# The score matmuls of an attention group and the first replacement of the search ahead of it: a change of order in a scheduled kernel

## The chip, the cores and the metric

The kernel runs on one core of a Trainium2 chip. The metric is the device time of one execution in microseconds (us). Three timed runs of the kernel before gave 1064.5, 1066.62 and 1068.95 us, median 1066.62. The profile is that of one further execution, which took 1060.82 us; its span from the first to the last instruction is 1059.1 us. The engines are named as the profile names them: PE is TensorE (matmuls), PEld its weight loads, DVE is VectorE, ACT is ScalarE, POOL is GpSimd, SP is SyncE, which issues most of the DMAs.

## The reference

Three layers follow each other; all is in float32.

```python
# attention: batch 4, 8 heads, 576 rows, head size 64; only the 32 highest scores of a row count
scores = q @ k.T / sqrt(64)
kth    = np.partition(scores, -32)[..., -32:-31]
scores = np.where(scores >= kth, scores, -1e9)
attn   = softmax(scores);  x = attn @ v          # x: 2304 tokens x 512
# a dense layer: 512 -> 2048 -> 512
h = x @ w_in;  x = (np.maximum(h, 0) + np.log1p(np.exp(-abs(h)))) @ w_out
# 8 experts, each token goes to the one with the highest gate
logits = x @ w_gate;  e = argmax(logits)
out = softmax(logits)[e] * (np.maximum(x @ w1[e], 0) @ w2[e])
```

## The kernel before

The program has two parts. `part_one` computes the attention, the dense layer and the routing of each token to its expert; `part_two` runs the experts, 256 token places at a time. The change is in `part_one`.

Attention is worked in 72 groups. A group is two tiles of 128 score rows x 576 keys. For a group, `emit_scores` issues two sets of matmuls through `emit_qk`: the first set gives keys 0 to 255 into the PSUM tile `sa`, which ScalarE copies to the SBUF tile `s` (L416); the second set gives the other 320 keys into the PSUM tile `sb`. Both sets are matmuls of line L406. There is one buffer of `sa` and one of `sb`. So the `sa` matmuls of a group wait for the copy L416 of the group ahead, and the `sb` matmuls wait for the copy L452 of the group ahead, which is the last reader of `sb`.

`emit_softmax` then finds the 32nd highest score of each row. Six VectorE instructions fold the scores pairwise (L446 to L451; L446 is the first and needs both `s` from L416 and `sb`), ScalarE copies `sb` to `s` (L452), and then VectorE alternates between taking the eight highest values (MAX8, L456 and L472) and replacing them by a very small number (MATCH_REPLACE8, L468), three times. The result `kth` goes to ScalarE (`kths`, L479), which with GpSimd makes the masked exponentials: L480 on ScalarE, L481 on GpSimd, the exponential L482 on ScalarE, then two 16-bit halves (L490 to L492) and a DMA transpose to `pT` (L494). Three groups later `emit_av` multiplies `pT` with v (L509, L511) and VectorE divides by the sums (L533 to L536).

When all groups of a set of token tiles are done, the set becomes a unit of the dense layer. `layer1` (L596) and `layer2` (L636) are TensorE's large matmuls; between them ScalarE computes exp and ln (L610, L611). Such a step has twelve L596 matmuls, followed later by two or four L636 entries, and the main loop emits 1.7 steps per attention group once units are ready; what is left over follows after the last group. The loads of q, k and v for later heads (L326), sums of their absolute values for a later check (L335) and their 16-bit halves (L367, L380) are made ahead of need on the same engines. The weights of the dense layer are decoded during the first groups on ScalarE, VectorE and GpSimd (L247 to L260). L664 to L705 route the finished tokens.

No order is written out by hand. The program is emitted in the order of the main loop in `part_one`, where `tc.high_priority(offset=...)` moves a block ahead in priority, and a scheduler with its own model of times decides the order in which instructions stand on each engine. On the chip an engine then works through its own list in that order, and waits wherever an operand or a buffer isn't there. `tc.issue_after` and `tc.add_manual_dep` are further edges for the scheduler. In the main loop (before) the part in question reads:

```python
        if i + 1 < n:
            with tc.high_priority(offset=A_SC):
                emit_scores(i + 1)
        if 0 <= i < n:
            with tc.high_priority(offset=AHEAD):
                emit_softmax(i)
```

with `A_SC` and `AHEAD` both 100. A second version of the same part, in which `flags` is None, is in the program for unusual inputs and is not run here.

Of the kernel before, what the change touches and what calls it, by code (L numbers as in the profile page):

```python
# [41 lines left out]
NEG = -3.0e38  # L42
# [38 lines left out]
A_SC = 100  # L81
# [119 lines left out]
def part_one(tc, ctx, q, k, v, w_in, w_out, const, ident, before, ones, iota_e, reg_e, wg, ids,  # L201
             ohcum, done, early, table, rows, flags, sums, w_sums, e_sums, kths):
    nc = tc.nc
# [186 lines left out]
        pair[m] = (q1, q2, kt, v16, sc)  # L390

    sc_t, pt_t, o_t, x_t = {}, {}, {}, {}
    tops, last_qk = [None], [None]

    def emit_qk(m, kind, ps, k0, k1):
        q1, q2, kt, v16, sc = pair[m]
        if kind == "tail":
            parts = [(8, 9, h, 64 * h, 64 * h + 64) for h in range(2)]
        else:
            t, h = kind  # L400
            parts = [(2 * t, 2 * t + 2, h, 0, 128)]

        for r0, r1, h, p0, p1 in parts:
            cs = slice(h * 64, h * 64 + 64)
            for qs, first in ((q1, True), (q2, False)):
                last_qk[0] = nc.tensor.matmul(ps[p0:p1], lhsT=qs[:, h, r0:r1, :].rearrange("p r d -> p (r d)"),  # L406
                                              rhs=kt[:, k0:k1, cs], start=first, stop=not first)

    PS, QS, US = 4 * D, 2 * D, D

    def emit_scores(gi):
        s = row.tile([128, 2, S], F32, name="s")
        pa = ps_s.tile([128, 2, PS], F32, name="sa")
        for i, x in enumerate(groups[gi]):
            emit_qk(*x, pa[:, i], 0, 4)
        nc.scalar.activation(s[:, :, :PS], pa, AF.Copy)  # L416
        pb = ps_s.tile([128, 2, 512], F32, name="sb")
        for i, x in enumerate(groups[gi]):
            emit_qk(*x, pb[:, i, :PS + US], 4, R)
        if flags is None:  # L420
            nc.scalar.activation(s[:, :, PS:], pb[:, :, :PS + US], AF.Copy)
        sc_t[gi] = s, pb

    def emit_softmax(gi):
        group = groups[gi]
        n = range(2)
        s2, ps = sc_t.pop(gi)
        s = [s2[:, i] for i in n]
        sc = [pair[g[0]][4] for g in group]
        flb = 1 if flags is None else FLB  # L430
        if gi % flb == 0:
            tops[0] = sm.tile([128, 2 * flb, 32], F32, name="mx", bufs=2)
        mx = tops[0][:, 2 * (gi % flb):2 * (gi % flb) + 2]
        kth = mx[:, :, 31:32]
        e = [row.tile([128, S], F32, name="e", bufs=3) for _ in n]
        bt = sm.tile([128, 2, 1], F32, name="bias")
        if flags is None:
            src = list(s)
            wk = [row.tile([128, S], F32, name="wk") for _ in n]
        else:  # L440


            gl = ps[:, :, PS + US:PS + US + QS]
            gh = row.tile([128, 2, QS], F32, name="gt", bufs=1)
            w2 = row.tile([128, 2, S], F32, name="wk", bufs=WKB)
            nc.vector.tensor_tensor(out=gl, in0=ps[:, :, :QS], in1=s2[:, :, :QS], op=ALU.max)  # L446
            nc.vector.tensor_tensor(out=gh, in0=ps[:, :, QS:PS], in1=s2[:, :, QS:PS], op=ALU.max)
            nc.vector.tensor_tensor(out=w2[:, :, :QS], in0=gl, in1=gh, op=ALU.max)
            nc.vector.tensor_tensor(out=w2[:, :, QS:PS], in0=gl, in1=gh, op=ALU.min)
            nc.vector.tensor_copy(w2[:, :, PS:PS + US], ps[:, :, PS:PS + US])  # L450
            nc.vector.tensor_tensor(out=w2[:, :, PS + US:], in0=ps[:, :, :PS], in1=s2[:, :, :PS], op=ALU.min)  # L451
            nc.scalar.activation(s2[:, :, PS:], ps[:, :, :PS + US], AF.Copy)  # L452
            src = [w2[:, i, :QS] for i in n]
            wide = (QS, QS, PS + US, S)
        for i in n:
            nc.vector.max(out=mx[:, i, 0:8], in_=src[i])  # L456
        if flags is not None:
            nc.scalar.activation(bt, mx[:, :, 0:1], AF.Copy, scale=-SCORE, bias=LN_ESC)
        else:
            for i in n:  # L460
                nc.vector.tensor_scalar(bt[:, i], mx[:, i, 0:1], sc[i][:, 4:5], LN_ESC, op0=ALU.mult, op1=ALU.add)
        if flags is None:
            for i in n:
                nc.scalar.activation(e[i], s[i], AF.Exp, bias=bt[:, i], scale=sc[i][:, 3:4])
        for j in range(3):
            for i in n:
                to = wk[i] if flags is None else src[i]
                nc.vector.match_replace(out=to, in_to_replace=mx[:, i, 8 * j:8 * j + 8], in_values=src[i],  # L468
                                        imm_value=NEG)
                src[i] = to if flags is None else w2[:, i, :wide[j + 1]]  # L470
            for i in n:
                nc.vector.max(out=mx[:, i, 8 * j + 8:8 * j + 16], in_=src[i])  # L472
        if flags is not None and gi % FLB == FLB - 1:
            g0 = 2 * (gi - FLB + 1)
            nc.vector.tensor_reduce(flags[:, g0:g0 + 2 * FLB], tops[0][:, :, 15:32:8], op=ALU.min, axis=AX.X)
        for i in n:
            if flags is not None:
                if i == 0:
                    nc.scalar.activation(kths[:, 2 * gi:2 * gi + 2], kth, AF.Copy, scale=K_UP)  # L479
                nc.scalar.activation(e[i], s[i], AF.Relu, bias=kths[:, 2 * gi + i], scale=-K_UP)  # L480
                nc.gpsimd.tensor_tensor(out=e[i], in0=s[i], in1=e[i], op=ALU.subtract)  # L481
                nc.scalar.activation(e[i], e[i], AF.Exp, bias=bt[:, i], scale=SCORE)  # L482
                continue
            mk = row.tile([128, S], F16, name="mk", bufs=1)
            nc.vector.tensor_scalar(mk, s[i], kth[:, i], None, op0=ALU.is_ge)
            nc.gpsimd.tensor_tensor(out=e[i], in0=e[i], in1=mk, op=ALU.mult)
        for i in n:

            p16 = row.tile([128, R, 2, D], F16, name="p16", bufs=PB if flags is not None else 2).rearrange("p r s d -> p (r s d)")
            nc.scalar.activation(p16[:, 0:S], e[i], AF.Copy)  # L490
            nc.gpsimd.tensor_tensor(out=p16[:, S:S + D], in0=e[i][:, S - D:], in1=p16[:, S - D:S], op=ALU.subtract)  # L491
            nc.gpsimd.tensor_tensor(out=p16[:, S + D:], in0=e[i][:, 0:S - D], in1=p16[:, 0:S - D], op=ALU.subtract)  # L492
            pT = row.tile([128, R, 128], F16, name="pT", bufs=2 * LAG)
            nc.sync.dma_start_transpose(out=pT, in_=p16)  # L494
            pt_t[group[i]] = pT
# [291 lines left out]
    n = len(groups)  # L787
# [4 lines left out]
    for i in range(-1, n + LAG):  # L792
        if i == -1:
            with tc.high_priority(offset=AHEAD):
                for m in range(RB):
                    prep_load(m)
                prep_scale(0)
        while done_prep < len(pairs) and when[done_prep] <= i:
            with tc.high_priority(offset=A_PREP):
                if to_scale:  # L800
                    prep_scale(to_scale.pop()[0])
                prep_split(done_prep)
                if done_prep + RB < len(pairs):
                    prep_load(done_prep + RB)
                if done_prep + 1 < len(pairs):
                    to_scale.append((done_prep + 1, i + SCALE))
            done_prep += 1
        if to_scale and to_scale[0][1] <= i:
            with tc.high_priority(offset=AHEAD):
                prep_scale(to_scale.pop()[0])  # L810
        if i == -1:
            decode_some(2)
        if i + 1 < n:
            with tc.high_priority(offset=A_SC):
                emit_scores(i + 1)
        if 0 <= i < n:
            with tc.high_priority(offset=AHEAD):
                emit_softmax(i)
            with tc.high_priority(offset=0):
                decode_some(DECR)  # L820
        j = i - LAG
        if j >= 0:
            with tc.high_priority(offset=A_AV), ExitStack() as behind_scores:
                if i + 1 < n:

                    behind_scores.enter_context(tc.issue_after(last_qk[0].ins))
                for x in groups[j]:
                    emit_av(*x)
            for u in units.get(j, []):
                started += 1  # L830
                ready.append((u, started))
        if ready or cur or behind or side:
            credit += MOER
            some_work(int(credit))
            credit -= int(credit)
# [270 lines left out]
```

## Time and profile before

| | before |
|---|---|
| median of the timed runs | 1066.62 us (1064.5 to 1068.95) |
| the profiled execution | 1060.82 us, span 1059.1 us |
| TensorE busy | 889.8 us, 84% |
| VectorE busy | 853.0 us, 81% |
| ScalarE busy | 801.3 us, 76% |
| GpSimd busy | 603.0 us, 57% |
| TensorE waiting at `sb` for L452 | 50.8 us, 16 times |
| VectorE waiting at L446 for L416 | 33.3 us, 18 times |
| mean granted TensorE clock | 0.935 of full speed |

The attention groups run from 18 us to about 700 us of the span. The dense layer starts on TensorE at 143 us and ends near 800 us, and the experts take the rest. Busy times of TensorE are modelled, since matmuls overlap. A row of the waits says which instruction waited for which other, how much in total, how often, and the longest. A row of the timeline has the start, the duration, the engine, the line and the operands, and in brackets how long the engine had stood idle and what ended that. A row of the windows has, for one stretch, the busy time of each engine, the granted clock of TensorE as a share of full speed, the share of the DMA engines in use and GB/s.

### The profile page before, as it was taken

What the parts mean: (1) busy time and instruction counts of PE and PEld (TensorE: products, weight loads), DVE (VectorE), ACT (ScalarE), POOL (GpSimd) and SP (SyncE); (2) the same over time, 40 slices, a digit from 0 to 9 for tenths busy, and PEclk for the clock granted to TensorE, in tenths of its full rate; (3) what the DMA queues carried; (4) which work ended last, traced back from release to release, by engine and by line L of the source; (5) the groups of instructions that cost most, each with busy time, mean ns of one, the idle gap of its engine ahead of it and who ended that gap; (6) DMA issues with size and microseconds to landing.
All of it is one profiled execution on the core that took longest, in us unless ns stands there. A gap on an engine that the chain in (4) does not pass through costs nothing.

```text
span 1059.1 us, 22197 instructions
## 1 busy us (share of the span) xinstructions
PE 889.8 (84%) x7146; PEld 659.0 (62%) x7146; DVE 853.0 (81%) x3021; ACT 801.3 (76%) x1866; POOL 603.0 (57%) x631
## 2 busy tenths in 40 slices
PE   1124379666989797998999999999999999999994
PEld 0012256344656565665666667666787999999993
DVE  5789999899988688997889999965357987777774
ACT  5889899888799678897998898863677655555553
POOL 3889898998678587776877877762001022111111
PEclk9986579777999989998999999999999999999998
DMA  7897898985889987659876755564301667766760
GB/s 189 202 216 165 201 202 176 200 173 100 129 117 171 124 131 136 108 85 150 156 155 113 116 85 98 80 93 124 112 11 32 164 214 240 246 221 220 234 213 24
DMA packets 295859, 156.97 MB, mean 148 GB/s; under 512 B 257524, under 2 KB 257652, under 8 KB 295732
## 3 DMA queue, kind: packets, MB, share of 16 engines
q1 hardware_dynamic: 292116, 145.73, 65.2%
q0 software_dynamic: 3616, 9.72, 2.6%
q8 instruction: 58, 0.95, 0.4%
q14 instruction: 69, 0.57, 0.2%
HBM read 77.89 MB, written 11.11 MB: 84 GB/s over the span
## 4 chain that ended last, share of the span: by engine, by line
PE 47%; DVE 13%; DMA 9%; ACT 8%; POOL 6%; issue 4%; SPq 1%; POOLq 0%; ACTq 0%; DVEq 0%
PE h L937 10%; PE y L950 9%; PE h L596 9%; PE y L636 8%; DVE mx L472 3%; PE y L633 3%; DVE wk L468 3%; POOL e L481 2%; DMA vn<-in_v_dram 2%; DMA kt<-st 2%; DMA pT<-p 2%; PE m L509 1%; PE sb L406 1%; POOL p L492 1%; ACT e L482 1%
## 5 line engine op out<-in xcount | busy, mean ns | idle before, releaser
L636 PE MATMUL y<-w_out_s,g 128*128 128x512 f32 x480 | 233.7, 610 | 5.3 <-ACT g L611 4.7
L596 PE MATMUL h<-xT,w_in_s 128*128 128x256 f16 (+1 forms) x1920 | 224.5, 267 | 9.1 <-POOL w_in_s L260 3.2
L596 PEld LDWEIGHTS <-w_in_s 128*128 128x128 f16 x1920 | 173.6, 100 | 70.2 <-issue 43.6
L481 POOL TENSOR_TENSOR e<-s,e 128x576 f32<-128x576 f32 x144 | 202.5, 1421 | 16.9 <-ACT e L480 16.5
L472 DVE MAX8 mx<-wk 128x8 f32<-128x128 f32 (+2 forms) x432 | 200.8, 500 | 0.1
L492 POOL TENSOR_TENSOR p<-e,p 128x512 f16<-128x512 f32 x144 | 167.3, 1162 | 0.0
L406 PEld LDWEIGHTS <-q 128*128 128x128 f16 (+1 forms) x640 | 56.1, 109 | 175.5 <-issue 127.6
L468 DVE MATCH_REPLACE8 wk<-mx,wk 128x128 f32<-128x128 f32 (+1 forms) x432 | 144.6, 341 | 0.1
L636 PEld LDWEIGHTS y<-w_out_s,g 128*128 128x128 f32 x480 | 83.7, 195 | 69.0 <-issue 57.6
L917 POOL DMA_INDIRECT out_dram<-ot,idx x19 | 19.5, 1028 | 175.7 <-DVE ot L916 172.9
L482 ACT ACTIVATE e<-e,bias 128x576 f32<-128x576 f32 x144 | 110.5, 768 | 11.0 <-POOL e L481 10.4
L406 PE MATMUL sa<-kt,q 128*128 128x256 f16 (+1 forms) x320 | 53.0, 305 | 77.0 <-DMA kt<-st 22.9
L937 PEld LDWEIGHTS h<-xT,wf 128*128 128x128 f32 x864 | 111.8, 191 | 5.3 <-ACT wf L898 0.2
L937 PE MATMUL h<-xT,wf 128*128 128x256 f32 x864 | 113.9, 283 | 0.0
L950 PE MATMUL y<-wf,hT 128*128 128x512 f32 x432 | 112.8, 398 | 0.0
L406 PE MATMUL sb<-kt,q 128*128 128x320 f16 (+1 forms) x320 | 63.1, 340 | 50.9 <-ACT s L452 50.8
L480 ACT ACTIVATE e<-s,kths 128x576 f32<-128x576 f32 x144 | 105.0, 766 | 0.9
L509 PEld LDWEIGHTS <-pT 128*128 128x128 f16 (+1 forms) x1440 | 88.2, 107 | 24.4 <-issue 18.3
L509 PE MATMUL m<-v,pT 128*128 128x65 f16 (+1 forms) x1440 | 95.2, 202 | 9.5 <-DVE x L536 4.9
L490 ACT ACTIVATE p<-e 128x576 f16<-128x576 f32 x144 | 97.4, 678 | 5.0 <-DMA pT<-p 4.3
L491 POOL TENSOR_TENSOR p<-e,p 128x64 f16<-128x64 f32 x144 | 46.1, 320 | 73.6 <-ACT p L490 72.2
L610 ACT ACTIVATE sa<-h 128x256 f32<-128x256 f32 (+1 forms) x160 | 56.3, 352 | 40.1 <-PE h L596 39.3
(213 smaller groups left out, 1817.1 us busy)
## 6 DMA issues: line engine op xcount, KB each, us to landing
w1r<-in_moe_w_dram SPq DMA_DIRECT2D x20, 1024.0 KB
w2r<-in_moe_w_dram SPq DMA_DIRECT2D x20, 1024.0 KB, 6.6
w<-in_moe_w_in_dram SPq DMA_DIRECT2D x16, 512.0 KB, 4.2
w<-in_moe_w_out_dram SPq DMA_DIRECT2D x16, 512.0 KB
rows<-xr SPq DMA_DIRECT2D x37, 128.2 KB, 2.7
qn<-in_q_dram SPq DMA_DIRECT2D x16, 288.0 KB, 3.6
kn<-in_k_dram SPq DMA_DIRECT2D x16, 288.0 KB, 3.1
vn<-in_v_dram SPq DMA_DIRECT2D x16, 288.0 KB, 4.7
```

What stands on the lines that cost most here:

```text
L406: last_qk[0] = nc.tensor.matmul(ps[p0:p1], lhsT=qs[:, h, r0:r1, :].rearrange("p r d -> p (r d)"), rhs=kt[:, k0:k1, cs], start=first, stop= ...
L468: nc.vector.match_replace(out=to, in_to_replace=mx[:, i, 8 * j:8 * j + 8], in_values=src[i], imm_value=NEG)
L472: nc.vector.max(out=mx[:, i, 8 * j + 8:8 * j + 16], in_=src[i])
L480: nc.scalar.activation(e[i], s[i], AF.Relu, bias=kths[:, 2 * gi + i], scale=-K_UP)
L481: nc.gpsimd.tensor_tensor(out=e[i], in0=s[i], in1=e[i], op=ALU.subtract)
L482: nc.scalar.activation(e[i], e[i], AF.Exp, bias=bt[:, i], scale=SCORE)
L492: nc.gpsimd.tensor_tensor(out=p16[:, S + D:], in0=e[i][:, 0:S - D], in1=p16[:, 0:S - D], op=ALU.subtract)
L509: nc.tensor.matmul(o[:, h, 0:D + 1], lhsT=pT(r), rhs=v16[:, h, c, 0:D + 1], start=r == 0, stop=r == R - 1)
L596: nc.tensor.matmul(hps[:, :n], lhsT=w_in_s[:, c, j, p, o:o + 128], rhs=xT[:, 0:len(u.tiles), r, c, :], start=m == 0, stop=m == 3 * KD - 1)
L636: nc.tensor.matmul(u.y[i], lhsT=g[:, cs], rhs=w_out_s[:, f, :], start=f == 0, stop=f == KF - 1)
L937: nc.tensor.matmul(h, lhsT=w1f[:, a, c, :], rhs=xT[:, b, c, :], start=n == 0, stop=n == 3 * KD - 1)
L950: nc.tensor.matmul(y[i], lhsT=hT[g][:, a, i * 128:i * 128 + 128], rhs=w2f[:, b, :], start=g == 0 and n == 0, stop=g == KF2 - 1 and n == 2)
```

## The change

Three edits. The first replacement of a group's search (L468 with `j == 0`, the later one of its two tiles) is remembered. Each `sb` matmul of the next group gets an edge to it, of the class NoSync: the scheduler puts the matmul behind that instruction in its plan, and no semaphore is added on the chip. And in the main loop the scores of group i + 1 are emitted behind the softmax of group i instead of ahead of it, with a priority offset of 160 instead of 100.

```diff
@@ emit_qk
-                last_qk[0] = nc.tensor.matmul(ps[p0:p1], lhsT=qs[:, h, r0:r1, :].rearrange("p r d -> p (r d)"),
+                last_qk[0] = mm = nc.tensor.matmul(ps[p0:p1], lhsT=qs[:, h, r0:r1, :].rearrange("p r d -> p (r d)"),
                                               rhs=kt[:, k0:k1, cs], start=first, stop=not first)
+                if behind_search[0] is not None and k0:
+                    tc.add_manual_dep(mm.ins, behind_search[0], mybir.DependencyInfo(
+                        mybir.DependencyClass.NoSync, mybir.DependencyReason.DATA), reason="scores behind a search")
@@ emit_softmax
-                nc.vector.match_replace(out=to, in_to_replace=mx[:, i, 8 * j:8 * j + 8], in_values=src[i],
-                                        imm_value=NEG)
+                mr = nc.vector.match_replace(out=to, in_to_replace=mx[:, i, 8 * j:8 * j + 8], in_values=src[i],
+                                             imm_value=NEG)
+                if j == 0 and flags is not None:
+                    behind_search[0] = mr.ins.name
@@ main loop
-        if i + 1 < n:
+        if i < 0:
             with tc.high_priority(offset=A_SC):
-                emit_scores(i + 1)
+                emit_scores(0)
         if 0 <= i < n:
             with tc.high_priority(offset=AHEAD):
                 emit_softmax(i)
+        if 0 <= i and i + 1 < n:
+            with tc.high_priority(offset=A_SC + 60):
+                emit_scores(i + 1)
+        if 0 <= i < n:
             with tc.high_priority(offset=0):
                 decode_some(DECR)
```

Every engine has the same instructions before and after; only their order differs, and the line numbers behind the edits are 3 or 5 higher. Three places follow. Groups are counted from 0.

ScalarE's list around the scores of group 38, before: L480 belongs to group 36, L416 is the copy of `sa` of group 38, and L452 the copy of `sb` of group 37.

```order
L480 ACTIVATE e<-s,kths 128x576 x2
L611 ACTIVATE g<-sa 128x256
L482 ACTIVATE e<-e,bias 128x576
L490 ACTIVATE p_5301<-e 128x576
L610 ACTIVATE sa,e_sums<-h 128x256
L416 ACTIVATE s<-sa 128x2x256
L482 ACTIVATE e<-e,bias 128x576
L611 ACTIVATE g<-sa 128x256
L452 ACTIVATE s<-sb 128x2x320
```

The same place after; L455 is the copy of `sb` of group 37 (L452 before), L419 the copy of `sa` of group 38 (L416 before).

```order
L485 ACTIVATE e<-s,kths 128x576
L616 ACTIVATE g<-sa 128x256
L485 ACTIVATE e<-s,kths 128x576
L455 ACTIVATE s<-sb 128x2x320
L461 ACTIVATE bias<-mx 128x2
L615 ACTIVATE sa,e_sums<-h 128x256
L616 ACTIVATE g<-sa 128x256
L487 ACTIVATE e<-e,bias 128x576
L380 ACTIVATE vs<-vn 128x9x64
L495 ACTIVATE p_5289<-e 128x576
L419 ACTIVATE s<-sa 128x2x256
```

The copy of group 37's `sb` stood behind the copy of group 38's `sa`, and stands ahead of it now.

ScalarE's list around the scores of group 64, before; L416 is the copy of `sa` and L452 the copy of `sb` of group 64, and the first L482 is the second exponential of group 62.

```order
L482 ACTIVATE e<-e,bias 128x576
L416 ACTIVATE s<-sa 128x2x256
L490 ACTIVATE p_9045<-e 128x576
L610 ACTIVATE sa,e_sums<-h 128x256
L611 ACTIVATE g<-sa 128x256
L479 ACTIVATE kths<-mx 128x2
L480 ACTIVATE e<-s,kths 128x576 x2
L666 ACTIVATE x2T<-h 128x512
L482 ACTIVATE e<-e,bias 128x576
L452 ACTIVATE s<-sb 128x2x320
```

The same place after: the first L419 is the copy of `sa` of group 64, the second that of group 65, and L455 the copy of `sb` of group 64.

```order
L419 ACTIVATE s<-sa 128x2x256
L487 ACTIVATE e<-e,bias 128x576
L615 ACTIVATE sa,e_sums<-h 128x256
L495 ACTIVATE p_9029<-e 128x576
L616 ACTIVATE g<-sa 128x256
L484 ACTIVATE kths<-mx 128x2
L485 ACTIVATE e<-s,kths 128x576 x2
L487 ACTIVATE e<-e,bias 128x576
L495 ACTIVATE p_9175<-e 128x576
L615 ACTIVATE sa,e_sums<-h 128x256
L419 ACTIVATE s<-sa 128x2x256
L455 ACTIVATE s<-sb 128x2x320
```

The second exponential of group 62 stood ahead of the copy of `sa` and stands behind it now, and the copy of `sb` of group 64 has moved behind the copy of `sa` of group 65.

TensorE's list just ahead of the `sb` matmuls of group 40, before; L596 is the last matmul of a step of the dense layer's first half, L636 its second half.

```order
L596 LDWEIGHTS w_in_s
L596 MATMUL h<-xT,w_in_s 128x128
L636 MATMUL y<-w_out_s,g 128x512 x2
L406 LDWEIGHTS q_5383
L406 MATMUL sb<-kt,q_5383 128x320
```

The same place after; L601 is L596 before, L669 are four transposes of the routing (L664 before).

```order
L601 LDWEIGHTS w_in_s
L601 MATMUL h<-xT,w_in_s 128x128
L669 MATMUL h<-ident,xr 128x128 x4
L406 LDWEIGHTS q_5383
L406 MATMUL sb<-kt,q_5383 128x320
```

Counted from the program's start, 612 matmuls of L596 and 98 of L636 stood ahead of these `sb` matmuls, and 600 and 96 stand there now. In 20 of the 34 groups 36 to 69 the `sb` matmuls stand 10 to 17 matmuls of L596 earlier than before; the difference appears 7 times (at groups 36, 40, 43, 47, 52, 55 and 67) and goes back to nearly nothing or to the other side in between. At groups 18, 19, 21 and 22, and at groups 6 to 12, the numbers are the same as before.

## Rows read from the trace of the kernel before

**Rows 1.** Windows, five stages: stretch, length, busy per engine, clock, DMA
```profile
0.00:140.00 140.00, 40.02 (x364) 25.60 (x364) 116.00 (x385) 113.57 (x227) 109.80 (x121) 0.79 0.85 195
140.00:290.00 150.00, 120.19 (x993) 79.97 (x994) 139.62 (x471) 130.05 (x298) 129.15 (x127) 0.85 0.81 161
290.00:500.00 210.00, 189.28 (x1648) 126.67 (x1647) 174.73 (x732) 173.21 (x435) 152.88 (x161) 0.93 0.81 128
500.00:700.00 200.00, 196.04 (x1765) 133.51 (x1765) 187.80 (x771) 178.81 (x428) 152.85 (x163) 1.00 0.66 113
700.00:1059.00 359.00, 344.24 (x2386) 293.22 (x2382) 234.87 (x665) 205.63 (x482) 58.29 (x60) 0.99 0.51 156
```

**Rows 2.** Waits, TensorE, 0 to 140 us: us in total, times, longest
```profile
PE sb L406 <- ACT s L452: 35.7, 9, 5.9
```

**Rows 3.** Waits, TensorE, 140 to 290 us
```profile
PE sb L406 <- ACT s L452: 11.2, 5, 3.4
```

**Rows 4.** Waits, TensorE, 290 to 500 us
```profile
PE sb L406 <- ACT s L452: 3.8, 2, 2.5
```

**Rows 5.** Timeline, 421 to 428 us, group 40
```profile
422.65 0.27 DVE L468 MATCH_REPLACE8 wk<-mx,wk 128x128 f32<-128x128 f32 x1
...
423.13 0.83 PE L596 MATMUL h<-xT,w_in_s 128*128 128x128 f16 x12
423.14 0.69 ACT L452 ACTIVATE s<-sb 128x640 f32<-128x640 f32 x1
...
423.80 1.94 PE L636 MATMUL y<-w_out_s,g 128*128 128x512 f32 x4
...
425.57 0.71 PE L406 MATMUL sb<-kt,q 128*128 128x320 f16 x4
```

**Rows 6.** Timeline, ScalarE, 404 to 418 us, groups 37 and 38
```profile
407.53 0.59 ACT L416 ACTIVATE s<-sa 128x512 f32<-128x512 f32 x1
...
408.98 0.70 ACT L452 ACTIVATE s<-sb 128x640 f32<-128x640 f32 x1
...
415.24 0.69 ACT L452 ACTIVATE s<-sb 128x640 f32<-128x640 f32 x1
```

**Rows 7.** Timeline, TensorE, 404 to 418 us, the same groups
```profile
409.73 0.70 PE L406 MATMUL sb<-kt,q 128*128 128x320 f16 x4 [1.29 <-ACT s L452]
...
415.99 1.19 PE L406 MATMUL sb<-kt,q 128*128 128x320 f16 x4 [2.54 <-ACT s L452]
```

**Rows 8.** Windows of 10 us, TensorE: length, busy, clock, DMA
```profile
370.00:380.00 10.00, 9.87 (x35) 0.57 0.69 116
...
410.00:420.00 10.00, 7.03 (x76) 0.83 0.77 121
```

**Rows 9.** Waits, VectorE, 290 to 500 us
```profile
DVE sb L446 <- ACT s L416: 16.6, 5, 9.5
```

**Rows 10.** Waits, VectorE, 500 to 700 us
```profile
DVE sb L446 <- ACT s L416: 8.7, 6, 3.2
```

**Rows 11.** Timeline, 500 to 510 us, group 49
```profile
508.48 0.78 ACT L482 ACTIVATE e<-e,bias 128x576 f32<-128x576 f32 x1
...
509.15 0.59 ACT L416 ACTIVATE s<-sa 128x512 f32<-128x512 f32 x1
...
509.77 0.43 DVE L446 TENSOR_TENSOR sb<-sb,s 128x256 f32<-128x256 f32 x1 [1.18 <-ACT s L416]
```

**Rows 12.** Timeline, ScalarE, 637 to 647 us, group 64
```profile
640.59 0.69 ACT L452 ACTIVATE s<-sb 128x640 f32<-128x640 f32 x1
```

**Rows 13.** Timeline, TensorE, 637 to 647 us, group 65
```profile
643.83 0.84 PE L406 MATMUL sb<-kt,q 128*64 128x320 f16 x6
```

**Rows 14.** Timeline, 365 to 371 us, group 34
```profile
367.40 0.68 ACT L335 ACTIVATE q<-vn 128x576 f16<-128x576 f32 x1 [7.90 <-DMA vn<-in_v_dram]
...
370.11 0.43 DVE L446 TENSOR_TENSOR sb<-sb,s 128x256 f32<-128x256 f32 x1 [9.47 <-ACT s L416]
...
370.13 1.01 PE L406 MATMUL sa<-kt,q 128*128 128x256 f16 x4 [6.34 <-ACT s L416]
```

More of the change, by code (lines that the diff above doesn't have):

```diff
@@ L392, in part_one @@
     sc_t, pt_t, o_t, x_t = {}, {}, {}, {}
-    tops, last_qk = [None], [None]
+    tops, last_qk, behind_search = [None], [None], [None]
     def emit_qk(m, kind, ps, k0, k1):
```

## The prediction, made before the result was known

> **What bounds the kernel now.** I read the busy times by stage first, then the waits of TensorE and VectorE in the same stages, and then the timeline where a wait names the line that the change touches. The stages show that the bound changes hands [rows 1]. Up to 290 us VectorE sets the pace: from 140 to 290 us it is busy 139.62 of 150 us, TensorE only 120.19. From 290 to 500 us neither is full (TensorE 189.28, VectorE 174.73 of 210 us): each waits in turn for the other, mostly through ScalarE. From 500 us TensorE is full, with 196.04 of 200 us up to 700 us at full clock, and after the last group it works off what is left, 344.24 of 359 us. No instruction is added or removed, so TensorE's work stays the same, and the end can move only by what the order does to the idle time of the engine that is full in a stage: VectorE up to 290 us, either of the two up to 500 us, TensorE after that.
>
> **The edge itself.** It has no semaphore, so it can't make an engine wait, and by the trace the chip already does what it asks. In group 40 the later first replacement ends at 422.65 + 0.27 = 422.92 us, the copy L452 that frees `sb` ends at 423.14 + 0.69 = 423.83 us, and the `sb` matmuls start at 425.57 us [rows 5]. The `sb` matmuls must wait for L452 in any case. The change therefore acts through the new lists alone, and I go through the places where these differ and something waits.
>
> **The waits that it is aimed at.** TensorE waits at `sb` for L452 50.7 us in all: 35.7 us before 140 us, 11.2 us from 140 to 290 us, 3.8 us from 290 to 500 us, none later [rows 2 to 4]. The first 35.7 us are worth nothing: until the first unit is complete TensorE has only scores and products with v to run, and its list there hardly changes. The 11.2 us are four or five waits at groups 18 to 22, where the same number of dense matmuls stands ahead of `sb` as before; nothing has been moved into the gap. They stay: 0. Were they all gone, VectorE's 150 - 139.62 = 10.4 us of idle time there would cap the gain; as the order stands I keep that end out of the sum, and the same order excludes a loss.
>
> The 3.8 us are two waits, 1.29 and 2.54 us, at groups 38 and 39 [rows 7]. Their cause is ScalarE's list: the copy L452 of group 37 stands behind the copy L416 of group 38 and so runs only at 408.98 us, and the next L452 runs at 415.24 us [rows 6]. In the new list L452 is back ahead of L416. The first wait goes whole (-1.3). Of the second about 0.8 us must stay, since TensorE came to it at 415.99 - 2.54 = 413.45 us and the copy of 0.69 us can't start before VectorE's folding of that group is done about then: -1.7. The stretch 410 to 420 us has a granted clock of 0.83 [rows 8]: a third of it ran at the lower of the two levels, 1.2 GHz, after these idle stretches. With TensorE busy 7.03 us there this is worth up to 1.2 us; I take -0.8. Together -3.8, between 0 (another wait is late next at the same place) and -5.0.
>
> **L416 ahead of an exponential.** In most groups the copy L416 of the coming group now stands ahead of the second exponential of an older group, instead of behind it. Where VectorE waits at L446 for L416, this gives back at most the start-to-start time of that exponential, 509.15 - 508.48 = 0.67 us, of a wait such as 1.18 us [rows 11]. From 290 to 500 us there are five such waits, 16.6 us, of which 9.47 us belong to a late load [rows 9 and 14]; the other four give at most 4 x 0.67 = 2.7 us. Both engines have idle time there, so I count half, -1.3, between 0 and -2.7. From 500 to 700 us there are six, 8.7 us [rows 10], at most 6 x 0.67 = 4.0 us of VectorE's time; but TensorE has only 200 - 196.04 = 4.0 us of idle time in the whole stretch and has to run the same list, so these are hidden behind its matmuls: 0. Against this stands `kths`, which waits for the end of the search and in some groups is ahead of L416: in 12 groups before, in 11 after. That is even.
>
> **A new inversion.** At group 64 the copy L452 has moved behind L416 of group 65, the very thing that went at 37. Before, that copy ended at 640.59 + 0.69 = 641.28 us and the next `sb` started at 643.83 us [rows 12 and 13], 2.55 us later. The copies and exponentials put ahead of it add about 1.5 to 2 us, so the margin mostly covers them: +0.5, between 0 and the 1.29 us that the same inversion cost at 38.
>
> **`sb` earlier against the dense layer.** In 20 of groups 36 to 69 the `sb` matmuls stand about one step of dense matmuls earlier. At group 40 twelve L596 (0.83 us) and two L636 (half of 1.94 us) have gone from ahead of them, 1.8 us, while they started 425.57 - 423.83 = 1.74 us after the copy that they need [rows 5]. So TensorE comes to them just as they are released. Such a difference appears 7 times, and each time TensorE can lose at most the shift less the margin, since after one wait it is in step again. Twelve wider L596 elsewhere cost about the same. I take 0.2 us a time, +1.5, between 0 and 7 x 1.7 = 11.9 us. What is queued behind a waiting `sb` are the products with v (now often one by one between the scores), and behind these VectorE's division.
>
> **The sum** against the profiled execution (span 1059.1 us, 1060.82 us in all): -3.8 - 1.3 + 0.5 + 1.5 = -3.1 us, thus 1057.7 us. That execution lies 5.8 us below the median of the runs, 1066.62 us; on the median's scale the forecast is 1063.5 us, and with the ends that can be met together 1058 to 1070 us. About 0.5%, 5.3 us, is what a measurement of this kernel can tell from no change: below 1061.3 us is faster, above 1071.9 us slower.
>
> **Rivals.** *The late load goes.* At 367.40 us ScalarE had stood 7.90 us before the magnitude L335 for a load of v, with L416 behind it; VectorE waited 9.47 us and TensorE 6.34 us [rows 14], and TensorE then ran 370 to 380 us at a clock of 0.57, so most of it at 1.2 GHz [rows 8], which costs up to 4.3 us more. If the new SyncE list brings that load in time, 6.34 + 4.3 = 10.6 us go: 1063.5 - 10.6 = 1052.9 us. Against it: the load is still issued behind the transposes of the same two groups, and L335 is still ahead of that L416.
>
> *TensorE isn't full from 500 to 700 us.* Its weight loads are busy only 133.51 of 200 us there [rows 1], and if its matmuls could close up, VectorE's 4.0 us would count: 1063.5 - 4.0 = 1059.5 us. Against it: its idle time there is 2%. The Trainium skill speaks for this rival ("Perfetto Trace Analysis", "Identifying the Most-Contended Engine"): busy time of matmuls is not a good measure of TensorE's headroom, weight-load share and useful operations are. By that rule VectorE, at 187.80 of 200 us, would be the engine to relieve here; no row of this trace decides it.
>
> *Slower: TensorE stands at `sb`.* If the margins at the seven places are gone, because ScalarE's copies are later in the new lists than the old ones suggest, each costs its whole 1.7 us, and from 500 us on nothing makes up for it: 11.9 instead of 1.5 us, 1063.5 + 10.4 = 1073.9 us, and up to 1077 us if the clock falls after some, as in 410 to 420 us. For it: where dense matmuls don't fill the gap, a wait at `sb` is 35.7 / 9 = 4.0 us long before 140 us and 2.2 us from 140 to 290 us [rows 2 and 3]. Against it: the margin at 40 is 1.74 and at 65 2.55 us. It decides once the copy L452 ends later than TensorE comes to `sb` at most of the seven.
>
> *It does nothing.* The order is another draw of the same kind and the gains and losses cancel: 1066.6 us.
>
> **Chances.** The forecast 35% (12 of these faster, 23 within 0.5%); the late load 15% (faster); TensorE not full 10% (8 faster, 2 within); TensorE at `sb` 30% (28 slower, 2 within); nothing 10% (within). Faster 35%, within 37%, slower 28%. The range from 1053 to 1077 us holds all but the tails of the first and the third rival.
>
> **What would show it.** Right: no wait of TensorE for L452 near the scores of group 38 and shorter ones at 39; the waits of groups 18 to 22 still there; VectorE's waits for L416 fewer after 290 us, with TensorE's 500 to 700 us window unchanged at about 196. Wrong: TensorE's wait for L452 after 290 us above 6 us (third rival); no wait of several us for the load of v (first); an end that moves with VectorE's waits after 500 us while TensorE's work closes up (second); or a shift that begins before 290 us, where I count nothing.

## The result, and the profile after

The changed kernel takes 1079.95 us (median of 4 runs, 1076.88 to 1080.89) against 1066.55 us for the kernel before on the same chip: a ratio of 1.012, with the interval 1.009 to 1.0149. It is 13.4 us slower where 3.1 us faster was forecast, and 3 us above the range's upper end.

The page after begins with the span, 19.6 us longer than that of before, and the busy times. Every engine has as many instructions as it had; TensorE's busy time, which is modelled, is 7.1 us longer (889.8 before) at a mean clock of 0.927 instead of 0.935. The three windows under it answer to the middle rows of [rows 1] (stretch, length, busy time and instructions of each engine, granted clock, DMA share, GB/s):

```profile
span 1078.7 us, 22221 instructions
...
PE 896.9 (83%) x7146; PEld 660.4 (61%) x7146; DVE 853.0 (79%) x3021; ACT 801.0 (74%) x1866; POOL 602.7 (56%) x631
```

```profile
140.00:290.00 150.00, 116.05 (x935) 75.73 (x933) 134.12 (x449) 130.60 (x296) 129.12 (x127) 0.82 0.79 158
290.00:500.00 210.00, 189.09 (x1722) 129.20 (x1721) 181.60 (x756) 172.80 (x437) 151.70 (x162) 0.96 0.85 130
500.00:700.00 200.00, 191.02 (x1640) 126.54 (x1637) 176.09 (x717) 168.62 (x403) 147.03 (x158) 0.98 0.71 112
```

From 500 to 700 us TensorE was busy 196.04 us before and is busy 191.02 us now, and VectorE and ScalarE lost with it (187.80 to 176.09 and 178.81 to 168.62): all three stand there more than before, so it isn't more work on one of them that costs the time. What the change was aimed at did happen. These are TensorE's waits for L455, and in one stretch for L419, 0 to 140, 140 to 290, 290 to 500 and 500 to 720 us, against [rows 2 to 4] (total, times, longest; L455 and L419 are L452 and L416 of before):

```profile
PE sb L406 <- ACT s L455: 38.4, 9, 7.5
...
PE sb L406 <- ACT s L455: 12.2, 4, 4.5
...
PE sa L406 <- ACT s L419: 13.2, 2, 7.1
PE sb L406 <- ACT s L455: 1.3, 1, 1.3
...
PE sb L406 <- ACT s L455: 1.6, 1, 1.6
```

After 290 us TensorE waits 2.9 us for L455, before 3.8: the waits at 38 and 39 are gone, one of 1.31 us is new at the scores of group 41 (441.54 us) and one of 1.64 us at those of group 62, and the sign of the third rival (above 6 us) has not come:

```profile
628.61 0.84 PE L406 MATMUL sb<-kt,q 128*64 128x320 f16 x6 [1.64 <-ACT s L455]
```

But VectorE's waits for L419, 290 to 500 and 500 to 700 us, are longer than the 16.6 and 8.7 us of before [rows 9 and 10]:

```profile
DVE sb L449 <- ACT s L419: 20.7, 4, 8.6
...
DVE sb L449 <- ACT s L419: 17.6, 7, 6.4
```

Two runs of experiment 1 below, with the lists of before and (but for a few places on TensorE) the changed ones, have 19.9 and 10.5 us against 15.4 and 12.8. So the longer waits up to 500 us are within what two executions of the same lists differ by; those behind 500 us come again, though smaller. The next question is what ScalarE stood at ahead of L419. Its waits from 500 to 745 us, of before and then of after:

```profile
ACT xh L556 <- DMA xT<-xh: 5.7, 3, 4.1
...
ACT vs L380 <- DMA v<-vs: 2.6, 2, 1.7
```

```profile
ACT xh L561 <- DMA xT<-xh: 11.3, 2, 5.9
...
ACT vs L380 <- DMA v<-vs: 4.7, 1, 4.7
...
ACT p L495 <- issue: 4.2, 1, 4.2
```

ScalarE waits for transfers that free its staging tiles (`xh`, `vs`, and by one of the experiments `p`), and works strictly in order. The timeline of the changed kernel at one of them shows the chain through four engines; SPq is SyncE's queue issuing transfers, and the bracket gives the idle time ahead and what ended it:

```profile
571.27 0.60 SPq L385 DMA_DIRECT2D v<-vs  x1
...
573.31 4.62 SPq L499 DMA_TRANSPOSE pT<-p  x2
...
578.68 0.68 ACT L380 ACTIVATE vs<-vn 128x576 f16<-128x576 f32 x1 [4.71 <-DMA v<-vs]
...
580.15 0.58 ACT L419 ACTIVATE s<-sa 128x512 f32<-128x512 f32 x1
...
580.29 2.35 PE L641 MATMUL y<-w_out_s,g 128*128 128x512 f32 x3 [2.05 <-ACT g L616]
...
580.76 0.43 DVE L449 TENSOR_TENSOR sb<-sb,s 128x256 f32<-128x256 f32 x1 [4.44 <-ACT s L419]
```

The transfer issued at 571.27 us or just after frees `vs` only at 578.68; ScalarE stands 4.71 us, the copy L419 behind it is late by as much, VectorE loses 4.44 and even TensorE, in its full stretch, 2.05 us. A transfer also ends ScalarE's waits at 408.05 us (8.57 us, before 3.62 at the same instruction) and 503.74 us (5.94, before 1.96); at 608.96 us (4.18, before none) the profile names no releaser. What may slow the transfers stands just ahead: at 569.0 us GpSimd issued the routing's indirect write of 128 token numbers into `table`. Its 128 pieces of 4 bytes are small, yet they land late; these are issues from 280 to 745 us with their number and the median from issue to landing, of before:

```profile
q<-st SPq DMA_TRANSPOSE x16, 7.2
...
table<-ids,dsti POOLq DMA_INDIRECT x12, 8.6
```

In the stretches of slow transfer behind such a write, single packets of 256 bytes take up to 4.4 us (4.1 before); the median of all is 0.018 us.

### The profile page after: what moved, and what is told of

Same layout as the page of the kernel before. It is cut to its first block, busy times and chain, and to the rows that moved or that the text cites. A ratio compares the mean times of both kernels' runs of the same rounds, so it can differ in the third digit from the quotient of the medians.

```text
span 1078.7 us, 22221 instructions
## 1 busy us (share of the span) xinstructions
PE 896.9 (83%) x7146; PEld 660.4 (61%) x7146; DVE 853.0 (79%) x3021; ACT 801.0 (74%) x1866; POOL 602.7 (56%) x631
## 4 chain that ended last, share of the span: by engine, by line
PE 43%; DMA 14%; DVE 13%; POOL 12%; ACT 8%; issue 6%; SPq 4%; POOLq 0%; ACTq 0%; DVEq 0%
PE h L946 8%; PE h L601 8%; PE y L959 8%; PE y L641 7%; POOL e L486 4%; PE y L638 3%; DVE mx L477 3%; DVE wk L471 2%; DMA q<-st 2%; POOL p L497 2%; DMA w<-in_moe_w_in_dram 2%; DMA v<-vs 2%; DMA xT<-xh 2%; DMA kt<-st 2%; PE sa L406 1%
## 5 line engine op out<-in xcount | busy, mean ns | idle before, releaser
L641 PE MATMUL y<-w_out_s,g 128*128 128x512 f32 x480 | 236.8, 619 | 6.2 <-ACT g L616 5.9
L601 PE MATMUL h<-xT,w_in_s 128*128 128x256 f16 (+1 forms) x1920 | 226.0, 267 | 9.4 <-ACT sa L615 5.5
L601 PEld LDWEIGHTS <-w_in_s 128*128 128x128 f16 x1920 | 172.9, 100 | 68.5 <-issue 46.3
L406 PE MATMUL sa<-kt,q 128*128 128x256 f16 (+1 forms) x320 | 57.3, 312 | 80.2 <-ACT s L419 24.4
L514 PE MATMUL m<-v,pT 128*128 128x65 f16 (+1 forms) x1440 | 100.8, 201 | 11.6 <-DVE x L541 7.0
L514 PEld LDWEIGHTS <-pT 128*128 128x128 f16 (+1 forms) x1440 | 89.3, 106 | 30.4 <-issue 23.6
```

The source lines that it names most:

```text
L406: last_qk[0] = mm = nc.tensor.matmul(ps[p0:p1], lhsT=qs[:, h, r0:r1, :].rearrange("p r d -> p (r d)"), rhs=kt[:, k0:k1, cs], start=first, ...
L514: nc.tensor.matmul(o[:, h, 0:D + 1], lhsT=pT(r), rhs=v16[:, h, c, 0:D + 1], start=r == 0, stop=r == R - 1)
L601: nc.tensor.matmul(hps[:, :n], lhsT=w_in_s[:, c, j, p, o:o + 128], rhs=xT[:, 0:len(u.tiles), r, c, :], start=m == 0, stop=m == 3 * KD - 1)
L641: nc.tensor.matmul(u.y[i], lhsT=g[:, cs], rhs=w_out_s[:, f, :], start=f == 0, stop=f == KF - 1)
```

## The experiments

**Theory D:** the indirect writes hold up other transfers, ScalarE waits for these with the scores' copy behind it, and the changed order meets them worse. **Theory P:** the order of scores and products on TensorE loses the time, transfers have no part. For each run I also summed TensorE's gaps over 0.25 us from the records, in the stretches 140:290, 290:500 and 500:745 us. These sums come from one execution each, and two executions of the same lists differ by up to some 4 us.

**1. The parts of the change.** Without the edge (lines of `emit_qk` taken out; the engines' lists stay but for a few places on TensorE):

```diff
-                if behind_search[0] is not None and k0:
-                    tc.add_manual_dep(mm.ins, behind_search[0], ...)
```

> The changed kernel without its edge; the moved call and the offset of +60 stay. Main theory (the edge holds back nothing; the +60 makes the loss): as the changed kernel, about 1080 us, within 0.5%. Rival (the edge itself costs, as an extra wait or as a later place of the scores): back at 1066.5 us.

Ratio to before 1.0133 (1.0103 to 1.0164): as the changed kernel. With the edge and the moved call, and the old offset (lists as before):

```diff
-            with tc.high_priority(offset=A_SC + 60):
+            with tc.high_priority(offset=A_SC):
```

> The changed kernel with its edge and its moved call, but with the offset back at 100 instead of 160. The lists of all five engines are then those of the kernel before. Main theory (the +60 alone makes the loss): 1066.5 us, within 0.5%. Rival (the edge costs): 1080 us.

1.0002 (0.9981 to 1.0023). The edge and the moved call do nothing; the offset of 160, by the lists that it makes, does all. TensorE's gaps are 32.6, 16.6 and 11.8 us without the edge, and 30.3, 23.4 and 6.0 with the old offset; in both pairs the changed order has 2 to 4 us more in the first stretch and 6 to 9 us more in the last; in the middle one the difference changes its sign.

**2. Without the indirect writes**, in both kernels; every index is out of bounds and skipped:

```diff
-   in_=ids[:, col:col + 1], in_offset=None)
+   in_=ids[:, col:col + 1], in_offset=None, bounds_check=0, oob_is_err=False)
```

> The changed kernel with the bounds check of the routing's indirect write set to 0, so that no token's number is written to the table (the experts then gather other rows; the order of all instructions stays). Theory D (ScalarE's waits for transfers make the loss, and the slow stretches of DMA are set off by this indirect write): in 140 to 740 us ScalarE's waits for DMAs of several us (8.6 at 408 us, 5.9 at 504, 4.7 at 579, 5.4 at 729) go, and the last product with the values comes at 715 to 725 us instead of 740.8. Theory D2 (the stretches come from the loads and transposes themselves): the stretches stay, and the last product with the values at 735 to 745. Theory P (the loss is the order of scores and products on TensorE, DMA has no part): 735 to 745 as well, and where the stretches go nevertheless, the distance to the same edit of the kernel before stays at 13 to 20 us.

> The kernel before with the same edit: the bounds check of the routing's indirect write is 0, so that the table isn't written. Theory D: the last product with the values at 705 to 718 us instead of 721.2, and the distance to the changed kernel with the same edit shrinks from 19.6 to under 8 us. Theory D2: 718 to 724, distance about 20. Theory P: distance 13 to 20 whatever the stretches do.

After: 1042.69 us, 0.9842 (0.9811 to 0.9873). Before: 1044.48 us, 0.9849 (0.9817 to 0.9882). The distance of 13.4 us is gone; the changed order now lies 1.8 us ahead, which the intervals don't tell from nothing. The last product with the values ends at 702.1 and 706.6 us (with the writes 740.8 and 721.2), that of the changed order earlier than any of the theories had it. What follows that product takes 337 to 339 us in these four runs and in those of experiment 3, so the experts' reading other rows doesn't show in the time. ScalarE's waits for DMAs in 140 to 740 us fall from 57.0 to 24.1 and from 46.9 to 31.0 us; that this sum is larger with the changed lists is not shown, since the two runs of experiment 1 have 47.8 without the edge and 51.6 with the old offset. The window of 500 to 700 us without the writes, of the changed kernel and of the one before:

```profile
500.00:700.00 200.00, 198.89 (x1782) 135.80 (x1781) 179.76 (x747) 170.80 (x409) 148.38 (x161) 1.00 0.61 110
```

```profile
500.00:700.00 200.00, 195.86 (x1766) 133.87 (x1765) 181.35 (x750) 173.31 (x413) 152.39 (x165) 1.00 0.62 109
```

In the one profiled execution of each, TensorE is busier with the changed lists, 198.89 against 195.86 us, as the second rival had it. Theory P is out: the lists are the same, and the loss has gone.

**3. Which writes.** Only six (560 to 745 us) or only seven (before 500 us) of the eighteen skipped, in either kernel:

```diff
+   **(dict(bounds_check=0, oob_is_err=False) if 7 <= len(scatters) <= 12 else {})
```

(`len(scatters) < 7` for the early ones.)

> The changed kernel, in which only the six indirect writes between 560 and 745 us leave the table unwritten (the experts gather other rows for those tokens); the order is the changed kernel's. TensorE's idle time (gaps over 0.25 us) in 290:500 and 500:745 was 20.8 and 12.6 us with all writes, 8.5 and 0.7 with none, and 20.1 and 3.4 in the kernel before. Theory D (each write costs where a transfer that ScalarE waits for meets it): 500:745 falls to 1 to 4 us while 290:500 stays at 16 to 24, and the time is 0.2 to 0.7% above before instead of 1.2. Theory P (the order of scores and products makes the late loss, and the writes only bring the rest): 500:745 stays at 10 to 13 us, the time 1.0 to 1.4% above before.

> The changed kernel, in which only the first seven indirect writes (before 500 us) leave the table unwritten. Theory D: TensorE's idle time in 290:500 falls from 20.8 to 8 to 11 us and that in 500:745 stays at 10 to 14; the time within 0.6% of before on either side. Theory P: 500:745 stays too, so that this run alone can't tell the two apart; with the run beside it, the two falls should add up to that without any write (1.6% below before).

> The kernel before, in which the same six indirect writes (between 560 and 745 us) leave the table unwritten; its order is that of before. In the changed kernel these six cost 1.0% of the time, in before all eighteen cost 1.5%. Theory D (what a write costs hangs on the transfer that meets it; of the six only the one at 704 us met a wait of several us here): the six cost 0 to 0.4%, TensorE's idle time in 500:745 stays at 3 to 5 us (3.4 before), and the whole difference between the kernels in that stretch is theirs. Rival (each write costs about the same anywhere, and the changed kernel's late loss has another cause besides): they cost a third of 1.5%, 0.5% or more, here too.

> The kernel before, in which the first seven indirect writes (before 500 us) leave the table unwritten. In the changed kernel these seven cost 2.0%. Theory D: here they cost 1.2 to 1.6%, nearly all that the eighteen cost, and TensorE's idle time in 290:500 falls from 20.1 to 8 to 11 us. Rival (the same price at each write): 0.5 to 0.7%.

Ratios to before, and TensorE's gaps summed over all that has been told (us):

```
table not written at    order     ratio (interval)           140:290  290:500  500:745
nowhere                 before    1                             29.6     20.1      3.4
nowhere                 changed   1.0120 (1.0090-1.0149)        33.4     20.8     12.6
six late places         before    0.9994 (0.9974-1.0014)        29.5     24.3      3.2
six late places         changed   1.0030 (1.0009-1.0050)        34.5     18.0      5.2
seven early places      before    0.9801 (0.9777-0.9824)        31.3     10.0      3.0
seven early places      changed   0.9927 (0.9904-0.9950)        35.7      7.5      8.9
any place               before    0.9849 (0.9817-0.9882)        33.5     10.0      4.0
any place               changed   0.9842 (0.9811-0.9873)        34.9      8.5      0.7
```

The seven early writes cost the two orders the same: 1 - 0.9801 = 2.0% before, 1.012 - 0.9927 = 1.9% changed. The six late ones cost before 0.06% and the changed order 1.012 - 1.003 = 0.9%, some 9.5 us of the 13.4. So most of the loss lies in the late six, which in the order before cost nothing that can be measured.

The traces show which transfers they meet. These are ScalarE's waits (us) within 15 us behind three of the late writes; of the runs with late writes, the changed ones are the changed kernel, that without its edge and that without the early seven, and those of before are the kernel before, the run with the old offset and that without the early seven:

| ScalarE waits at | changed, late writes | before, late writes | changed, none late | before, none late |
|---|---|---|---|---|
| `vs`, behind the first | 4.71, 3.72, 3.71 | 0.87, 0.60, none | 0.80, 0.71 | none, none |
| `p`, behind the second | 4.18, 2.79, 2.52 | 0.36, 0.83, 0.60 | none, none | none, none |
| the last `xh`, behind the fifth | 5.35, 5.46, 5.68 | 4.12, 3.71, 2.85 | 2.46, 2.45 | 2.01, 1.96 |

(The 2.52 us at `p` end with the transfer `pT<-p` by the profile; for the other two of that row it names no releaser.) So each time the late writes stand in the changed order, ScalarE loses some 12 to 14 us at these three places, in the order before 3 to 5. TensorE's gap of 3.0 to 3.3 us ahead of the product with `wg`, behind the last `xh`, is in these three changed runs and in no other of the table.

Theory D holds by place and, for the late six, by size; its size at the early seven of before was set too low (1.2 to 1.6%), and the six left 5.2 us of gaps where 1 to 4 were expected. The changed order without the early seven missed three times: gaps of 7.5 us in 290:500 (8 to 11 expected) and 8.9 in 500:745 (10 to 14), and a time 0.73% below before (within 0.6%). The two falls do add up, 0.9 and 1.9% against 2.8% without any write. Not explained: in the order before, leaving out seven writes gained more (2.0%) than leaving out all eighteen (1.5%). The two intervals just overlap, and in the profiled executions part of it lies ahead of the first write, which comes at about 280 us: the 200th matmul L596 started at 259.2 us with seven left out and at 262.1 with eighteen.

**4. Why a write of half a kilobyte is slow.** Successive places of an expert are neighbouring 4-byte words. The number's index times 16 puts each 64 bytes behind the last (table 1.2 MB, cleared at the start; the experts' reading follows; the lists shift a little); a second pair also writes 64 bytes each time. Of the edit, the index:

```diff
-    table = dram.tile([E * NT + SLOT, 1], I32, name="table")
+    table = dram.tile([(E * NT + SLOT) * 16, 1], I32, name="table")
...
-        nc.vector.tensor_copy(dsti, dst)
+        nc.vector.tensor_scalar(dsti, dst, 16.0, None, op0=ALU.mult)
```

> The kernel before with the table of token numbers spread: each number stands 64 bytes behind the one ahead (the index is multiplied by 16), so that the successive places of one expert no longer lie side by side; the writes stay 4 bytes and 128 in number. The table to be cleared grows from 75 KB to 1.2 MB, and the program's order shifts a little with it. Theory L (numbers side by side write to the same few bytes of memory and wait for each other, and other transfers behind them): the slow stretches go, ScalarE's waits for DMAs in 140 to 740 us fall from 46.9 to about 25 to 32 us, and the time is 1040 to 1052 us on a chip where before takes 1060 to 1066. Theory S (each 4-byte write is slow wherever it goes): stretches and waits stay, 1060 to 1072.

> The changed kernel with the same spread table. Theory L: 1038 to 1052 us, within 6 us of the kernel before with the spread table, as without the writes (distance there 1.8). Theory S: 1075 to 1085, the distance of 13 to 20 us stays.

> The kernel before with the spread table, and each write 64 bytes long (the number 16 times) instead of 4. Theory L: as with the spread table and 4-byte writes, within 0.5%. Theory S (a short write is slow because the memory must read before it writes): only here the stretches go, 1040 to 1052 us, while the spread 4-byte writes stay at 1060 to 1072.

> The changed kernel with the same 64-byte writes. If the writes of 64 bytes no longer slow other transfers (theories L and S): 1038 to 1052 us, within 6 us of the kernel before with 64-byte writes. If any indirect write of 128 pieces sets off the stretches: 1075 to 1085, 13 to 20 us behind it.

Before, spread: 1046.03 us, 0.9868 (0.985 to 0.9886); with 64-byte writes 1048.92, 0.9901 (0.9882 to 0.9921). Changed: 1055.33, 0.9964 (0.994 to 0.9988), and 1054.79, 0.995 (0.9921 to 0.9979). ScalarE's waits for DMAs are 29.0, 23.6, 28.6 and 27.1 us, as without any write. The same issues as above, of before with the spread table:

```profile
q<-st SPq DMA_TRANSPOSE x16, 3.0
...
table<-ids,dsti POOLq DMA_INDIRECT x13, 3.2
```

The write lands in 3.2 instead of 8.6 us, and the transposes of q in 3.0 instead of 7.2. Distance cures it and length adds nothing: against theory S, and as theory L has it; what in the memory does it no run shows. The Trainium skill ("DMA: Bandwidth & Descriptors", "Back-pressure in remote DMA") says, of writes between cores, that stalled writes also stall the other queues of the DMA engine that they come from. Here other queues' transfers are slower beside one core's writes to its own memory (7.2 against 3.0 us); that they stall in the same way no run shows.

The distance between the orders was to be within 6 us. It is 9.3 us with 4-byte and 5.9 us with 64-byte writes: the first misses, and both times of the changed order lie above the 1038 to 1052 us that were expected. The last product with the values is level there (709.0 and 708.5 us, 4-byte), but TensorE's gaps in 140:290 are 35.0 before and 42.1 changed, and behind that product the changed order has 22 matmuls of the dense layer's first half and 4 of its second more left over (343.5 us to the end against 337.5). These lists aren't those of the plain kernels, so this says nothing on the 13.4 us; it shows that an order can lose in that stretch too, and that without slow transfers the changed order is not the better one in general.

**5. A version that beats both.** The clearing moved behind the first unit's dense layer:

> The kernel before with the spread table (64 bytes from number to number, 4-byte writes), and the clearing of its 1.2 MB moved from the program's start behind the first tiles' dense layer, some 250 us in. With the clearing at the start the first products of the dense layer came 7 us late (152.8 us instead of 145.3). If that delay is the clearing's: 1038 to 1044 us on a chip where before takes 1059. If 290 us on has no room for 1.2 MB either: 1044 to 1052.

> The changed kernel with the same two edits. If the changed order is worth what it was without the writes: 0 to 4 us below the kernel before with the two edits; with its loss of 5 to 7 us in 140 to 290 us, as in the run with the spread table and early clearing: 3 to 9 us above it.

```diff
+                if u.number == 1 and i == 0:
+                    side.append(clear_table())
```

Before with both edits 1045.57 us, 0.9844 (0.9825 to 0.9864), 16 us faster than before on that chip; its first dense matmul starts at 148.6 us instead of 152.8. That is less than the whole delay (145.3), and the time lies in the upper of the two expected ranges (1044 to 1052). The changed order with them 1049.55 us, 0.9868 (0.9842 to 0.9893), 4 us behind, at the lower end of what was expected with the early loss. That the late clearing is better than the early one (0.9868) the intervals just don't settle.

## Why the prediction was wrong

- **The edge itself**: right, both ways (experiment 1).
- **The waits that it is aimed at**: right in kind. The two at 38 and 39 are gone and those at 18 to 22 stayed (11.2 to 12.2 us). Net of the two new ones at 41 and 62, TensorE's wait for L455 after 290 us fell by 0.9 us.
- **L416 ahead of an exponential**: this is the step that failed. It priced a wait for L416 by the one instruction that changed places ahead of it (0.67 us each, -1.3 in all) and took what ScalarE itself waits for as given. But the long waits for L416 come from the transfers at which ScalarE stands, and the new order meets other ones: ScalarE's waits behind the late writes are 12 to 14 us instead of 3 to 5 (experiment 3), and VectorE's waits for L416 in 500 to 700 us, forecast to fall, are 17.6 and 12.8 us in two executions against 8.7 and 10.5. Leaving out the late writes alone takes back 0.9% of the 1.2% lost, some 9.5 us. The only term that touched a transfer was the first rival, and that let one late load go, not others come. At 372 us it is still there with 6.68 us (7.90 before).
- **"From 500 to 700 us ... hidden behind its matmuls: 0"**: failed with it. Two per cent of idle time is no cover against 4 to 6 us of ScalarE standing, since TensorE's list also holds products that wait for ScalarE; its gaps in 500 to 745 us rose from 3.4 to 12.6 us (6.0 and 11.8 in the two runs of experiment 1). Nor was the stretch full in the other direction: without the writes the changed order brings them to 0.7. The Trainium skill's rule on headroom ("Perfetto Trace Analysis", "Identifying the Most-Contended Engine") would have relieved VectorE there; no run relieves it, so the rule stays untested here. These gaps closed by order alone, with VectorE busy 181.35 us before and 179.76 after.
- **A new inversion** (+0.5, at most 1.29): it cost nothing. The `sb` matmuls of group 65 start 2.26 us after the copy that they need, without a wait. **`sb` earlier** (+1.5, up to 11.9): at none of the seven places did TensorE wait, though at 40, 43 and 47 it came 0.05 to 0.13 us after the copy. The new waits are 1.31 us at 41, in all five runs with the changed lists, and 1.64 us at 62, in the three of them with late writes alone. The slower time that the third rival stood for came by another cause.
- **Nothing before 290 us**: off by about 3 us, ahead of any indirect write. The first dense matmul starts at 143.4 to 145.3 us in five profiled runs with the lists of before and at 146.0 to 148.4 with the changed ones (means 144.3 and 147.0), behind longer waits at `sb`, the 35.7 us that were called worth nothing (38.4 now). The 200th matmul L596 started at 256.5, 257.4, 262.1, 258.6 and 259.2 us in the same five runs of before, mean 258.8, and at 262.7, 262.0, 261.5, 260.8 and 262.2, mean 261.8, with the changed ones: still 3 us. Whether it is made up later no pair shows: of the two runs without writes, the one with the order of before was itself at 262.1.
- **The sum**: -3.1 us for the order on its own. With the writes out it is -1.8 us by the medians, within the noise, and TensorE's three gaps give 44.1 - 47.5 = -3.4: neither refuted nor shown, and with the spread table, where the lists are others, the changed order is 9.3, 5.9 and 4.0 us behind. What was missing is a term for the transfers, of 9.5 us by the late writes and of 13.4 + 1.8 = 15.2 us by all.

## What to carry to other kernels

Before pricing a new order by the waits that it moves, list what the in-order engines wait for that isn't an engine: each single staging tile freed by a transfer is a place where a slow transfer stops everything behind it, and a new order can draw these meetings anew. If the trace holds stretches where small packets take microseconds, remove their cause first; until then a difference of order of one per cent may measure the collisions, as it mostly did here. Here the cause was a scatter to neighbouring words, and 64 bytes between them were worth more than the whole change.

## What the hardware showed that I had not expected

- One indirect write of 128 x 4 bytes to neighbouring words takes 8.6 us to land (the median of 12), and the transposes of q from 280 to 745 us take 7.2 us by the median; 64 bytes apart it takes 3.2 us, and they take 3.0.
- All eighteen cost 1.5% of the time in one order and 2.8% in another (1.012 - 0.9842), with the same instructions.
- SyncE's issue of one transpose, 1.3 us by the median, took up to 5.0 us in the changed kernel after 500 us (2.3 before).
- The DMA share of busy time tells little: in the changed kernel it was 0.71 from 500 to 700 us with the writes and 0.61 without, while TensorE's gaps from 500 to 745 us went from 12.6 to 0.7 us.
